# First attention batch: v's loads move to SyncE's queue, strided rows keep the mask's order, VectorE multiplies by the reciprocal sums

## The chip, the cores and the metric

The program runs on one core of one Trainium2 chip. The metric is the device time of one execution in microseconds (us); the time before is 892.8 us, the median of three runs. The engines are called TensorE (PE, with its weight loads PEld), VectorE (DVE), ScalarE (ACT), GpSimd (POOL) and SyncE (SP, which only issues transfers). The 16 DMA engines of the core are shared by all queues.

## What is computed

The reference is sparse attention followed by two MLPs, all in float32 accuracy:

```python
scores = q @ k.T / sqrt(64)                     # 4 batches, 8 heads, 576 positions, head size 64
mask_local   = (rel >= 0) & (rel < 32)          # heads 0 to 3
mask_strided = (rel >= 0) & (pos_k % 32 == pos_q % 32)   # heads 4 to 7
attn = softmax(where(mask, scores, -1e9)) @ v
x = attn as (2304 tokens, 512)
x = ((x @ w_a) * (x @ w_b)) @ w_out             # 512 -> 1536 -> 512
h = x @ w_in; y = (h * sigmoid(h)) @ w_out2     # 512 -> 2048 -> 512
```

## The kernel before, in words

**The whole.** The MLPs are a long chain of blocks on TensorE; the attention of batches 1 to 3 is woven into those blocks by a plan. Ahead of the first block stands a start-up part, which computes the attention of batch 0 alone and converts the first weights. This change touches only that part (and one tile that later batches read).

**The stages of the start-up.** A loop runs `s` from -1 upwards. The nine units of batch 0 enter one by one: units 0 to 4 are the local heads (a window of 128 positions each, the last one 64), units 5 to 8 the strided heads (`RES` lists which residues modulo 32 belong to each). In stage `s`, unit `s` gets its scores (S: TensorE, `scores`, L459 writes the mask and L466 adds q times k) and its row maxima (L: VectorE, `largest`, L488); unit `s-1` gets its exponentials (X: ScalarE, L500), 1e-9 on the sums (G: VectorE, L523) and the reciprocal and the product with it (N: `normalise`, L527 on VectorE, L538 on GpSimd); unit `s-3` is transposed (T: TensorE, L558) and copied back (U); unit `s-5` is multiplied with v (V: TensorE, `values`, L607) and stored to `x` (O: L636 on ScalarE, L639 on VectorE). `ORDER = "AXPV0QWS1LGRTBKUON2Y"` is the order of these steps inside a stage, and every engine works through its own instructions in exactly that order. Letter K puts matmuls on constants (L885) on TensorE; `WARM1` gives their number for each stage.

**Conversion of weights.** The weights come as 64-bit words of 512 KB a piece. For the first six pieces, `CONV` says in which stage a piece is converted: B (ScalarE, L701), 0 (GpSimd, L739), 1 (VectorE, L747), 2 (VectorE, L752); in the next stage Y splits it in two parts (ScalarE L774, VectorE L775). `PART` says in which stage TensorE multiplies the first half of a block with them (A, L782).

**Loads.** `LOADS` is a list by stage; capital letters go to ScalarE's queue, small ones to SyncE's, in the order written. `q`, `k` with a number are the local heads' pairs, `t8` the eight transfers of the strided q and k (L311: `qld`, `kld`, 128 bytes a row), `m7` the strided mask (six transfers L910, each a third of 54 rows, in the order of residues), `s` the sixteen transfers of the strided v (L395, tile `vs`), `w` a piece of weights (L673, L675), `u` q and k of batch 1. The local v (tile `vl`, ten transfers, L365 and L375) is issued by GpSimd in its own queue, ahead of the stage loop. Name `b` turns the strided mask into bfloat16 (L915, GpSimd), and `R` in stage 3 makes the scaled strided queries of units 5 and 6 (L427, GpSimd, six instructions).

**The order around the change.** On GpSimd, stage 3 has the mask's cast (L915), then the six query scalings, then the product of unit 2; stage 4 has that of unit 3. On VectorE, stage 4 has two transposes of the strided k (L325). On TensorE, stage 5 has the values of unit 0, the scores of unit 5, then the transpose of unit 2.

Of the kernel before, what the change touches and what calls it, by code (L numbers as in the profile page):

```python
# [9 lines left out]
F32 = mybir.dt.float32  # L10
F32R = mybir.dt.float32r
BF16 = mybir.dt.bfloat16
# [5 lines left out]
ALU = mybir.AluOpType  # L18
# [21 lines left out]

LOADS = {
    -2: (
        "q0 Q1 i M1 k0 K1 K2 Q2 t8 m7 s2 w0 s2 s1 w2 s2 s1 w1 s1 s1 s1 w4 "
        "w3 s5 u2 u5 u2"
    ),
    3: "b",
    8: "w5 w6",
    10: "w7",
    11: "w11",
    12: "w8 w9",  # L50
# [8 lines left out]
EVAC = "dada"  # L59
TURN_D = (0, 3, 5, 8)  # L60

CONV = {5: 0, 8: 1, 10: 2, 11: 3, 13: 4, 14: 5}
PART = {11: 0, 12: 1, 15: 2, 16: 3}

EARLY = len(CONV)
# [63 lines left out]
def attention_gated_mlp_silu_mlp(  # L129
# [55 lines left out]

    ident = cpool.tile([P, P], F32, name="ident")
    ident_b = cpool.tile([P, P], BF16, name="ident_b")
    lead.tile([P, 32], F32, name="lead")
    mask_loc = apool.tile([P, 4, HALF], BF16, name="mask_loc", bufs=1)
    mask_str = apool.tile([P, JR], BF16, name="mask_str", bufs=1)  # L190

# [80 lines left out]
    class Batch:  # L272
# [125 lines left out]
        def prepare(self, u):  # L398
# [20 lines left out]
            else:  # L419
                res = RES[i]  # L420
                ng = len(res)
                st = dict(w=JR, segs=2 * ng, slots=ng, n=J * (res[-1] - res[0] + TAKE))
                st["mask"] = mask_str.unsqueeze(1).to_broadcast([P, 2 * ng, JR])
                qh = queries[i % 2]
                if self.first:
                    for g, r0 in enumerate(res):
                        nc.gpsimd.tensor_scalar_mul(  # L427
                            qh[:, :, g, :JR].rearrange("p c (r j) -> p c r j", r=TAKE),
                            qT.rearrange("p c (j r) -> p c r j", r=STRIDE)[:, :, r0:r0 + TAKE],
                            SCALE,  # L430
                        )
                parts = []
# [96 lines left out]
        def normalise(self, u):  # L529
            ty, i = self.units[u]  # L530
            st = self.state[u]
            segs, w, ng = st["segs"], st["w"], st["slots"]
            rs = st["rs"]
            if self.first:
                self.invert(u)
            pr, rs = st["pr"][:, :ng, :, :w], rs.rearrange("p (i g) -> p g i", i=2)
            rs = rs.unsqueeze(3).to_broadcast([P, ng, 2, w])
            nc.gpsimd.tensor_tensor(out=pr, in0=pr, in1=rs, op=ALU.mult)  # L538

        def shared(self, us):  # L540

# [32 lines left out]
        def values(self, *us):  # L574
# [6 lines left out]
            for u in us:  # L581
                i, st = self.units[u][1], self.state[u]
                pt = st["pt"]
                for g in range(st["slots"]):
                    for k in range(2 if ty == 0 else 1):
                        for hp in range(2):
                            for c in range(2):
                                rows = slice(HALF * c, HALF * (c + 1))
                                if ty == 0:
                                    keys = slice(HALF * hp, HALF * (hp + 1))  # L590
                                    parts.append((
                                        banks[hp][rows, o + STRIDE * k:][:, :STRIDE],
                                        self.vl[keys, 2 * i + g, k, c, :],
                                        pt[keys, g, 2 * k + c, :],
                                    ))
                                else:
                                    r0 = RES[i][g]
                                    keys = slice(HALF * hp, HALF * hp + JR)
                                    out = banks[hp][rows, :first["cols"]].rearrange("p (j r) -> p r j", j=J)
                                    parts.append((  # L600
                                        out[:, r0 - RES[self.units[us[0]][1]][0]:][:, :TAKE],
                                        vs[keys, firsts.index(r0), c, :],
                                        pt[keys, P * g + HALF * c:P * g + HALF * c + JR],
                                    ))
                    o += HALF
# [270 lines left out]
    with tc.manual_schedule():  # L876
# [11 lines left out]
        nu = len(batch.units)  # L888
        every = lambda loads: [None for _ in loads]
        after = Batch(1, False)  # L890
        qs0, vs0, q1 = batch.load_qk(1), batch.load_vs(), after.load_qk(0)

        masks = [epool.tile([P, n], F32, tag="e", name="mask") for n in (5 * HALF, JR)]
        masks[0] = masks[0].rearrange("p (s k) -> p s k", k=HALF)
        nc.gpsimd.memset(masks[1], 0.0)

        def startup_loads(names):

            for name in names.split():
# [5 lines left out]
                elif name[0] == "m" and n == 1:  # L905
                    feed[0].dma_start(out=masks[0], in_=mask_loc_d)
                elif name[0] == "m":
                    for h in range(0, P, HALF):
                        for r in range(TAKE):
                            feed[0].dma_start(  # L910
                                out=masks[1][h + J * r:h + J * (r + 1)],
                                in_=mask_str_d[h:h + JR].rearrange("(j r) k -> r j k", r=TAKE)[r],
                            )
                elif name[0] == "b":
                    nc.gpsimd.tensor_copy(out=mask_str, in_=masks[1])  # L915
                elif name[0] in "qk":
                    batch.load_pair(n, "qk".index(name[0]))
                elif name[0] == "w":
                    load_words(n)
                else:  # L920
                    for _ in range(n):
                        next({"t": qs0, "s": vs0, "u": q1}[name[0]], None)

            feed[0] = nc.sync

# [3 lines left out]
        nc.gpsimd.tensor_copy(out=ident_b, in_=ident)  # L929
        for s in range(0, 4, 2):  # L930
            nc.gpsimd.tensor_copy(out=mask_loc[:, s:s + 2], in_=masks[0][:, :2])
        feed[0] = nc.gpsimd
        every(batch.load_vl())
        feed[0] = nc.sync
        keep_warm(WARM0)
        partial = {}
        for s in range(-1, max(nu + LV, max(PART), max(CONV) + 1) + 1):
# [690 lines left out]
```

## Time and profile before

| what | value |
|---|---|
| median of 3 runs | 892.8 us (892.75 to 893.99) |
| the profiled execution's own time | 891.74 us |
| its span, first to last instruction | 890.0 us |
| TensorE matmul busy | 876.0 us, 98% |
| VectorE, ScalarE, GpSimd busy | 71%, 61%, 18% |
| end of the last constant matmuls and start of solid block work on TensorE | about 44 us |

The profile is of one execution. A time in it counts from the first instruction; idle time before an instruction is written in brackets, with what ended it. When an instruction waits for several things, the one that came last by the profile is named, and a DMA can stand behind another name. [...]

### The profile page before, as it was taken

The numbers are of one execution on the slowest core, as the hardware profiler recorded it, in microseconds if no ns is written. First come the engines' busy times: TensorE is split into PE (matmuls) and PEld (weight loads), VectorE is DVE, ScalarE is ACT, GpSimd is POOL, SyncE is SP. The second block draws the span as 40 slices with busy tenths as digits, with TensorE's granted clock in tenths as the row PEclk, the third lists the DMA queues.
The fourth block names the chain that finished last, engine by engine and source line by source line (L and its number), as shares of the span: only waits on it lengthen the run. The fifth ranks groups of instructions, "written<-read, shape, count | busy, mean of one in ns | idle before, by whom it ended". The sixth has DMA issues, their size and how long they took to land.

```text
span 890.0 us, 16103 instructions
## 1 busy us (share of the span) xinstructions
PE 876.0 (98%) x5859; PEld 728.6 (82%) x5866; DVE 633.4 (71%) x1175; ACT 542.7 (61%) x1296; POOL 162.2 (18%) x232
## 2 busy tenths in 40 slices
PE   8799999999999999999999999999999999999998
PEld 5578788888887788899888888888888888898987
DVE  4687877767667665888776768776777697766664
ACT  4779898676786756675444344755554565455553
POOL 5664564444433110100000000000000000000000
PEclk9899999999999999999999999999999999999999
DMA  9999999798999922664122122321121242311201
GB/s 185 220 252 294 281 282 295 228 288 266 311 301 269 304 82 95 190 190 143 47 72 62 57 71 71 115 75 59 60 72 53 93 162 71 132 59 51 80 1 71
DMA packets 152977, 133.77 MB, mean 150 GB/s; under 512 B 91522, under 2 KB 114690, under 8 KB 152898
## 3 DMA queue, kind: packets, MB, share of 16 engines
q1 hardware_dynamic: 143986, 108.59, 43.4%
q0 software_dynamic: 7424, 23.34, 7.2%
q8 instruction: 46, 0.75, 0.3%
q10 hardware_dynamic: 1488, 0.82, 0.3%
q14 instruction: 33, 0.27, 0.1%
HBM read 110.16 MB, written 22.54 MB: 149 GB/s over the span
## 4 chain that ended last, share of the span: by engine, by line
PE 86%; DVE 5%; ACT 4%; DMA 2%; issue 1%; POOL 1%; SPq 1%; POOLq 0%; ACTq 0%; DVEq 0%
PE ring L782 17%; PE acc L1167 13%; PE ring L1103 12%; PE att L1103 9%; PE ring L1167 7%; PE att L1167 7%; PE acc L1103 7%; PE acc L1538 6%; PE acc L1566 3%; PE att L607 1%; ACT prs L500 1%; PE acc L885 1%; PE att L466 1%; DMA vs<-in_v_dram 1%; DVE w L775 1%
## 5 line engine op out<-in xcount | busy, mean ns | idle before, releaser
L1432 DVE TENSOR_TENSOR w<-raw,w 128x512 fp32r<-128x512 f32 (+1 forms) x164 | 103.2, 641 | 14.8 <-ACT w L1431 14.1
L782 PE MATMUL ring<-x1a,w 128*128 128x256 f32 (+1 forms) x480 | 99.0, 327 | 0.0
L1431 ACT CAST w<-raw 128x512 fp32r<-128x512 f32 (+1 forms) x164 | 93.1, 581 | 7.3 <-ACT w L1431 3.0
L1103 PE MATMUL ring<-L,w 128*128 128x512 f32 x360 | 87.8, 389 | 0.0
L1216 POOL DMA_DIRECT2D out_dram<-o x12 | 6.5, 543 | 407.8 <-DVE o L1215 398.9
L1103 PEld LDWEIGHTS ring<-L,w 128*128 128x128 f32 x360 | 67.6, 188 | 14.0
L1167 PE MATMUL acc<-w,h 128*128 128x512 f32 x288 | 78.5, 391 | 0.0
L782 PEld LDWEIGHTS ring<-x1a,w 128*128 128x128 f32 x480 | 71.5, 190 | 7.7
L775 DVE TENSOR_TENSOR w<-raw,w 128x512 fp32r<-128x512 f32 x80 | 61.6, 777 | 14.2 <-ACT w L774 14.1
L1538 PE MATMUL acc<-h,w 128*128 128x512 f32 x288 | 70.5, 394 | 0.6 <-ACT h L792 0.4
L792 ACT CAST h<-h 128x512 fp32r<-128x512 f32 (+1 forms) x48 | 27.2, 567 | 71.9 <-DVE h L1140 40.5
L1538 PEld LDWEIGHTS acc<-h,w 128*128 128x128 f32 x288 | 53.2, 188 | 12.4 <-ACT h L792 0.6
L1167 PEld LDWEIGHTS acc<-w,h 128*128 128x128 f32 x288 | 53.6, 188 | 9.4 <-DVE h L793 0.4
L727 POOL TENSOR_SCALAR raw<-words 128x512 f16<-128x512 uint8 x56 | 51.8, 926 | 42.5 <-DMA words<-in_moe_w_out_dram 9.8
L782 PE MATMUL ring<-x,w 128*128 128x512 f32 x240 | 58.2, 394 | 0.3 <-DVE w L775 0.3
L1167 PE MATMUL acc<-h,w 128*128 128x256 f32 (+1 forms) x288 | 53.5, 336 | 0.0
L782 PEld LDWEIGHTS ring<-x,w 128*128 128x128 f32 x240 | 44.3, 188 | 10.6 <-DVE w L775 1.6
L1167 PE MATMUL ring<-w,h 128*128 128x512 f32 x192 | 51.9, 391 | 0.0
L774 ACT CAST w<-raw 128x512 fp32r<-128x512 f32 x80 | 49.2, 623 | 1.3 <-DMA raw<-keptp 1.3
L1167 PEld LDWEIGHTS acc<-h,w 128*128 128x128 f32 x288 | 45.2, 190 | 5.7
L793 DVE TENSOR_TENSOR h<-h,h 128x512 fp32r<-128x512 f32 (+1 forms) x48 | 30.9, 643 | 26.4 <-ACT h L792 26.4
L1167 PE MATMUL att<-w,h 128*128 128x512 f32 x192 | 49.3, 391 | 0.0
(263 smaller groups left out, 1908.6 us busy)
## 6 DMA issues: line engine op xcount, KB each, us to landing
raw<-keptp SPq DMA_DIRECT2D x64, 256.0 KB
words<-in_moe_w_out_dram SPq DMA_DIRECT2D x28, 512.0 KB
raw<-kepti SPq DMA_DIRECT2D x48, 256.0 KB
raw<-kepto SPq DMA_DIRECT2D x45, 256.0 KB
words<-in_moe_w_in_dram SPq DMA_DIRECT2D x16, 512.0 KB
raw<-keptb SPq DMA_DIRECT2D x32, 256.0 KB
raw<-kepta SPq DMA_DIRECT2D x31, 256.0 KB
words<-in_moe_w_a_dram SPq DMA_DIRECT2D x12, 512.0 KB
```

What stands on the lines that cost most here:

```text
L727: nc.gpsimd.tensor_scalar(out=halves_of(made[c], F16, 1), in0=bytes_of(words[c], 8, 7), scalar1=-TINY, scalar2=127.5 * TINY, op0=ALU.mult, ...
L774: nc.scalar.copy(out=o[:, 0], in_=t)
L775: nc.vector.tensor_tensor(out=o[:, 1], in0=t, in1=o[:, 0].bitcast(F32), op=ALU.subtract)
L782: nc.tensor.matmul(ps[:, :T], lhsT=w[:, wi, c * P:(c + 1) * P], rhs=x[:, xi, c, :T], start=(c == 0 and wi == 0 and xi == 0), stop=(c == CC ...
L792: nc.scalar.copy(out=o[:, 0, :T], in_=t32[:, :T])
L793: nc.vector.tensor_tensor(out=o[:, 1, :T], in0=t32[:, :T], in1=o[:, 0, :T].bitcast(F32), op=ALU.subtract)
L1103: nc.tensor.matmul(self.acc[acc], lhsT=w[:, wi, (2 * part + c) * P:(2 * part + c + 1) * P], rhs=x[:, xi, c], start=(begin and c == 0 and m ...
L1167: nc.tensor.matmul(o, lhsT=lhsT, rhs=rhs, start=(first and wi == 0 and xi == 0), stop=(last and wi == 1))
L1431: nc.scalar.copy(out=o[:, 0, cols], in_=t)
L1432: nc.vector.tensor_tensor(out=o[:, 1, cols], in0=t, in1=o[:, 0, cols].bitcast(F32), op=ALU.subtract)
L1538: nc.tensor.matmul(accs[d], lhsT=w[:, wi, d * P:(d + 1) * P], rhs=h[:, xi], start=(j == 0 and wi == 0 and xi == 0), stop=(j == N1 - 1 and ...
L1566: nc.tensor.matmul(accs[t][:, :DM], lhsT=h[:, xi, t * P:(t + 1) * P], rhs=w[:, wi, :], start=(j == 0 and wi == 0 and xi == 0), stop=(j == ...
```

## The change

- The ten transfers of v (local heads, batch 0) leave GpSimd's queue. SyncE issues them behind the strided q and k and the mask.
- The strided mask comes in one transfer of 128 rows, in the order in which it lies in memory (position major, residue minor). It is cast into a tile `mask_first` that lies in 128 bytes a row that were an empty pad. The scaled queries of batch 0 and the columns that `values` writes follow that order.
- Later batches still want the residue-major order: in stage 8 six small transfers inside the chip (name `c`) copy the rows of `mask_first` into `mask_str` in that order.
- In batch 0 the product with the reciprocals (L538) is VectorE's instead of GpSimd's.
- The cast `b` moves from stage 3 to stage 4. Pieces 1 and 2 of the weights are converted in stages 7 and 9 instead of 8 and 10. The order of the loads of `vs` and of the weights changes: piece 1 ahead of piece 2, all of `vs` ahead of piece 2.

```diff
 LOADS = {
     -2: (
-        "q0 Q1 i M1 k0 K1 K2 Q2 t8 m7 s2 w0 s2 s1 w2 s2 s1 w1 s1 s1 s1 w4 "
-        "w3 s5 u2 u5 u2"
+        "q0 Q1 i M1 k0 K1 K2 Q2 t8 m7 v9 v1 w0 s2 s2 w1 s4 s4 s4 w2 w4 "
+        "w3 u2 u5 u2"
     ),
-    3: "b",
-    8: "w5 w6",
+    4: "b",
+    8: "w5 w6 c",
-CONV = {5: 0, 8: 1, 10: 2, 11: 3, 13: 4, 14: 5}
+CONV = {5: 0, 7: 1, 9: 2, 11: 3, 13: 4, 14: 5}
-    lead.tile([P, 32], F32, name="lead")
+    mask_first = lead.tile([P, 64], BF16, name="lead")[:, :JR]
@@ prepare
-                st["mask"] = mask_str.unsqueeze(1).to_broadcast([P, 2 * ng, JR])
+                rows = mask_first if self.first else mask_str
+                st["mask"] = rows.unsqueeze(1).to_broadcast([P, 2 * ng, JR])
-                            qh[:, :, g, :JR].rearrange("p c (r j) -> p c r j", r=TAKE),
-                            qT.rearrange("p c (j r) -> p c r j", r=STRIDE)[:, :, r0:r0 + TAKE],
+                            qh[:, :, g, :JR].rearrange("p c (j r) -> p c j r", r=TAKE),
+                            qT.rearrange("p c (j r) -> p c j r", r=STRIDE)[..., r0:r0 + TAKE],
@@ normalise
-            nc.gpsimd.tensor_tensor(out=pr, in0=pr, in1=rs, op=ALU.mult)
+            engine = nc.vector if self.first else nc.gpsimd
+            engine.tensor_tensor(out=pr, in0=pr, in1=rs, op=ALU.mult)
@@ values
-                                    out = banks[hp][rows, :first["cols"]].rearrange("p (j r) -> p r j", j=J)
+                                    out = banks[hp][rows, :first["cols"]].rearrange("p (j r) -> p j r", j=J)
+                                    out = out[..., r0 - RES[self.units[us[0]][1]][0]:][..., :TAKE]
                                     parts.append((
-                                        out[:, r0 - RES[self.units[us[0]][1]][0]:][:, :TAKE],
+                                        out if self.first else out.rearrange("p j r -> p r j"),
@@ start-up
-        nc.gpsimd.memset(masks[1], 0.0)
+        nc.gpsimd.memset(mask_str, 0.0)
                 elif name[0] == "m":
+                    feed[0].dma_start(out=masks[1], in_=mask_str_d)
+                elif name[0] == "c":
                     for h in range(0, P, HALF):
                         for r in range(TAKE):
                             feed[0].dma_start(
-                                out=masks[1][h + J * r:h + J * (r + 1)],
-                                in_=mask_str_d[h:h + JR].rearrange("(j r) k -> r j k", r=TAKE)[r],
+                                out=mask_str[h + J * r:h + J * (r + 1)],
+                                in_=mask_first[h:h + JR].rearrange("(j r) k -> r j k", r=TAKE)[r],
                             )
                 elif name[0] == "b":
-                    nc.gpsimd.tensor_copy(out=mask_str, in_=masks[1])
+                    nc.gpsimd.tensor_copy(out=mask_first, in_=masks[1])
-        feed[0] = nc.gpsimd
-        every(batch.load_vl())
-        feed[0] = nc.sync
```

## Rows read from the trace of the kernel before

**Rows 1.** Stretches: us, busy by engine, TensorE's granted clock, DMA share, GB/s.

```profile
20.00:25.00 5.00, 2.72 (x60) 1.83 (x62) 1.95 (x6) 1.59 (x7) 4.57 (x9) 1.00 0.74 204
25.00:30.00 5.00, 4.18 (x95) 2.91 (x95) 3.61 (x16) 4.15 (x26) 3.46 (x6) 0.61 0.95 214
40.00:45.00 5.00, 4.00 (x52) 2.70 (x52) 5.00 (x19) 2.68 (x11) 1.80 (x2) 1.00 1.05 254
...
54.80:97.40 42.60, 42.54 (x322) 34.02 (x322) 33.23 (x60) 37.52 (x94) 22.17 (x28) 1.00 0.99 268
```

**Rows 2.** DMA share in tenths, 10 to 26 us in 40 slices of 0.4 us.

```profile
DMA  9999999999998999999961032024469999989979
```

**Rows 3.** DMA queues, 6 to 10 us (first row), then 10 to 18 us.

```profile
q1 hardware_dynamic: 4174, 0.58, 103.9%
...
DMA packets 5598, 1.77 MB, mean 222 GB/s; under 512 B 5281, under 2 KB 5343, under 8 KB 5597
q1 hardware_dynamic: 5155, 0.65, 60.7%
q0 software_dynamic: 442, 1.10, 60.0%
```

**Rows 4.** Timeline of SyncE: start, length, line, tile, count of issues.

```profile
8.07 5.56 SPq L311 DMA_DIRECT2D kld<-in_k_dram  x4
13.75 4.01 SPq L910 DMA_DIRECT2D mask<-in_mask_str_dram  x6
18.47 1.60 SPq L395 DMA_DIRECT2D vs<-in_v_dram  x2
20.12 0.40 SPq L675 DMA_DIRECT2D words<-in_moe_w_a_dram  x1
```

**Rows 5.** Timeline of GpSimd.

```profile
7.81 5.64 POOL L375 DMA_DIRECT2D vl<-in_v_dram  x8
23.86 1.17 POOL L538 TENSOR_TENSOR prs<-prs,rs 128x256 f32<-128x256 f32 x2
25.11 0.64 POOL L739 TENSOR_SCALAR x<-words 128x512 int32<-128x512 uint8 x1
```

**Rows 6.** Timeline of ScalarE.

```profile
24.35 0.68 ACT L701 ACTIVATE e<-words 128x512 f32<-128x512 f32 x1 [2.11 <-DMA words<-in_moe_w_a_dram]
26.55 0.31 ACT L500 ACTIVATE prs<-acc,nm 128x54 f32<-128x54 f32 x1 [0.85 <-DVE nm L488]
```

**Rows 7.** Timeline of VectorE.

```profile
19.90 1.44 DVE L325 STREAM_TRANSPOSE kT<-kld 128x576 f32<-128x576 f32 x2 [1.32 <-DMA mask<-in_mask_str_dram]
25.79 0.46 DVE L747 TENSOR_SCALAR x<-words 128x512 uint8<-128x512 uint8 x1 [3.81 <-POOL x L739]
34.38 0.46 DVE L747 TENSOR_SCALAR x<-words 128x512 uint8<-128x512 uint8 x1 [1.69 <-POOL x L739]
39.74 0.46 DVE L747 TENSOR_SCALAR x<-words 128x512 uint8<-128x512 uint8 x1 [1.19 <-POOL x L739]
```

**Rows 8.** Timeline of TensorE.

```profile
19.98 0.25 PE L607 MATMUL att<-ptl,vl 64*64 64x32 f32 x2
...
21.26 1.48 PE L466 MATMUL acc<-kT,qs 64*64 64x54 f32 x24 [0.25 <-POOL qs L427]
24.51 0.44 PE L558 MATMUL ring<-ident,prs 128*128 128x128 f32 x2 [1.78 <-POOL prs L538]
...
97.60 0.73 PE L782 MATMUL ring<-x,w 128*128 128x512 f32 x2 [0.26 <-DVE w L775]
```

**Rows 9.** Groups by line and shape: count | busy us, mean ns | idle.

```profile
L639 DVE TENSOR_TENSOR x1b<-att,x1a 128x256 fp32r<-128x256 f32 x2 | 0.7, 415 | 0.0
L775 DVE TENSOR_TENSOR w<-x,w 128x512 fp32r<-128x512 f32 x4 | 2.7, 674 | 0.1
L427 POOL TENSOR_SCALAR qs<-qT 128x108 f32<-128x108 f32 x11 | 6.8, 635 | 0.1
```

**Rows 10.** Timeline of VectorE at 92 us, GpSimd reading memory at the time.

```profile
92.61 1.10 DVE L775 TENSOR_TENSOR w<-raw,w 128x512 fp32r<-128x512 f32 x1
```

More of the change, by code (lines that the diff above doesn't have):

```diff
@@ L890, in attention_gated_mlp_silu_mlp @@
         after = Batch(1, False)
-        qs0, vs0, q1 = batch.load_qk(1), batch.load_vs(), after.load_qk(0)
+        qs0, vs0, v0, q1 = batch.load_qk(1), batch.load_vs(), batch.load_vl(), after.load_qk(0)
         masks = [epool.tile([P, n], F32, tag="e", name="mask") for n in (5 * HALF, JR)]
         masks[0] = masks[0].rearrange("p (s k) -> p s k", k=HALF)
-        nc.gpsimd.memset(masks[1], 0.0)
+        nc.gpsimd.memset(mask_str, 0.0)
         def startup_loads(names):
@@ L921, in startup_loads @@
                     for _ in range(n):
-                        next({"t": qs0, "s": vs0, "u": q1}[name[0]], None)
+                        next({"t": qs0, "s": vs0, "u": q1, "v": v0}[name[0]], None)
             feed[0] = nc.sync
```

## The prediction

> **What bounds the kernel now.** I read the table by stretches first, then the timelines of the queues and engines over the first 50 us, then the ramp behind them. From 54.8 to 97.4 us TensorE is busy 42.54 of 42.60 us [rows 1], so behind the start-up the matmuls are the bound, and time can only be won ahead of them. There the worst stretch is 20 to 25 us: TensorE 2.72 of 5 us, VectorE 1.95, ScalarE 1.59, while GpSimd is busy 4.57 [rows 1]. The reader is to see three engines waiting for GpSimd and for transfers. TensorE waits 1.78 us at 24.51 for the product of unit 2 [rows 8]; VectorE waits 3.81 us up to 25.79 for the first weight's conversion on GpSimd, and ScalarE 2.11 us up to 24.35 for the first weight's transfer [rows 6, 7]. Just ahead of it the DMA engines fall nearly idle: the strip is full to 18.0 us, then at 0 to 6 tenths until 22.0 us [rows 2]. SyncE explains the hole: it is at the strided k until 13.63 us, at six tiny mask transfers until 17.76 us, and the first weight goes out at 20.12 us [rows 4]. So the start-up is a queue, not a sum of work: strided k and mask are late, GpSimd stands in order behind the mask, and the first weight is late.
>
> Later the limit changes hands. From 40 to 45 us VectorE is busy 5.00 of 5 [rows 1].
>
> **Part 1, v behind q and k on SyncE.** Removed from GpSimd: ten issues, of which the last eight take 5.64 us from 7.81 [rows 5]. GpSimd has nothing else then (its next work waits for the first reciprocal), so this is worth nothing. What counts is the order of the transfers. The strided q and k are 9,216 pieces of 128 bytes (2 tensors, 4 heads, 576 rows, two halves). With SyncE's queue nearly alone, 4,174 packets moved from 6 to 10 us, 1,044 a microsecond; with v beside it, 5,155 in 8 us, 644 a microsecond, while v's queue took 60.0% of the engines' time [rows 3]. Behind the change the second part goes at the first rate: 5,155 / 1,044 = 4.9 us, done at 14.9 us, instead of running to the thin end of the strip at 18.4 [rows 2]. The gain in k itself is small, because VectorE came to its transposes only at 18.6 us and began them at 19.90, after 1.32 us of waiting [rows 7]; the three products that it now does before them (1.2 us, priced below) eat that.
>
> v is 1.18 MB. At the mean 222 GB/s of 10 to 18 us [rows 3] it takes 5.3 us: drained at 20.2, landed at 20.2 to 21.7 (the last k was used 1.5 us after the strip thinned out at 18.4 [rows 2, 7]); I take 21.0. TensorE began unit 0's values at 19.98 [rows 8], so this is a new wait of 1.0 us. Queued behind it on TensorE: scores of unit 5, transpose of unit 2. Both wait less than before: unit 5's matmuls took 1.48 us at 21.26 because the scaled queries came in drops, and the 1.78 us for the product are gone [rows 8]. From the values' start to unit 5's first matmul it took 1.28 us, 0.25 of them waiting [rows 8]. So 21.0 + 1.0 + 1.2 (estimate: the 1.48 less the drops) = 23.2, and the transpose starts there instead of at 24.51: the new wait is covered by 1.3 us. The cover is gone if v lands after 22.3.
>
> **Part 2, one mask transfer.** Five issues and their room in the queue go, 4.01 us from 13.75 [rows 4]. With them goes the hole: v and the weight stand right behind. The first weight (0.52 MB) at the 214 GB/s of 25 to 30 us [rows 1] takes 2.5 us behind v: 22.7, landed at 23.2 with 0.5 us for the landing (bounds: 21.3 with v and weight at the 268 GB/s of the ramp and no tail, 24.8 with both at the 204 GB/s of 20 to 25 us and a tail of 1.5 [rows 1]). It was used at 24.35 [rows 6].
>
> **Part 3, the cast and the queries on GpSimd.** Six scalings at 0.635 us [rows 9] from VectorE's second query transpose (about 18.1, an estimate: just ahead of its idle time that began at 18.58 [rows 7]) end at 21.9, then the narrow cast, some 0.2: 22.1. The scores of unit 5 want that at about 21.7, a loss of 0.4 us that the cover above holds. The new pattern of the scaling has runs of 3 instead of 18; no row shows its price. Bounds: 0.64 x 108/512 = 0.14 us from the 512-wide conversion [rows 5], and twice 0.635; I take 0.635. The slow bound would put the scores at 25.9 and take the gain away.
>
> **Part 4, products on VectorE.** GpSimd loses them, so the first conversion no longer stands behind 1.17 us of products; it started at 25.11 [rows 5] and can start at 23.3, when the weight is there. VectorE's next step, at 25.79 [rows 7], then starts at 23.3 + 0.64 + 0.06 = 24.0. **Main term: 25.79 - 24.0 = 1.8 us** (bounds 0.3 to 3.8 by the landing of the weight). Unit 5's maxima stand right behind it on VectorE, and ScalarE's exponentials of unit 5, at 26.55 [rows 6], move with them. The price on VectorE: 415 ns for 256 columns, 674 ns for 512 [rows 9], so about 1.0 ns a column and 0.16 fixed: 0.42 x 4 + 0.29 + 0.49 x 3 + 0.38 = 3.8 us for nine, of which five, 2.1 us, fall after 25 us. They go into idle time: VectorE waits 1.69 us at 34.38 and 1.19 us at 39.74 for conversions that stood behind products on GpSimd [rows 7], 2.9 us together. ScalarE is near solid behind 26.55 (4.15 of 5 from 25 to 30 [rows 1]) and caps what is won. Net 0.8 by VectorE; I count **0.5 us** (bounds -2.1, if neither wait shrinks, to 0.8).
>
> **Part 5, the rest.** Pieces 1 and 2 convert a stage earlier: same instructions, ahead of VectorE's full stretch; 0. Their new order in the queue puts piece 2 behind all of `vs`, but everything in the queue is some 3 us earlier (the hole); 0. Six small copies in stage 8 are issues on SyncE at 0.67 us each (4.01 / 6 [rows 4]), 4 us at most, when its next weights are for pieces converted stages later; 0, covered by those stages. Memset and pad: 0.
>
> **Sum.** 1.8 + 0.5 = 2.3 us, kept to the end: VectorE's full stretch from 40 us only begins earlier, and behind it TensorE is full [rows 1]. Against the profiled execution 891.74 - 2.3 = 889.4; the median lies 1.06 above that execution, so 890.5.
>
> **The rivals.**
>
> *Given back in the ramp.* TensorE waited 0.26 us at 97.60 for a split [rows 8], and from 54.8 to 97.4 the DMA share is 0.99 and ScalarE works 37.52 of 42.60 us [rows 1]. If weights can't come earlier, blocks that begin 2.3 us earlier wait there: 892.8 less at most 0.5, 892.5. Against it: the hole is filled, so transfers come earlier too.
>
> *VectorE pays.* Each of the seven products beside GpSimd work may also be held up by a reading instruction there, as the split was: 1.10 - 0.67 = 0.43 us each, 3.0 us in all, and VectorE is full from 40 us [rows 1]. Gain 2.3 - 3.0 = -0.7: 893.5. The split's 1.10 us against 674 ns [rows 9, 10] speak for it; against it, the waits on GpSimd at 34.38 and 39.74 are larger than the products. The Trainium skill, "SBUF — State Buffer", section "Who interferes with whom", states the rule behind it: a VectorE instruction with two SBUF inputs contends with a GpSimd instruction that reads SBUF, and whichever comes second waits for the whole of the other. By that rule, the sum is the 893.5 of this rival if every product comes second, and the 890.5 of the forecast if none does; the slow split agrees with it.
>
> *v late (slower).* Place: values of unit 0, at the head of TensorE's order, with the weight behind v in the same queue. If v's 4,608 pieces of 256 bytes go at 500 a microsecond instead of 870 (1.18 MB at 222 GB/s), v takes 9.2 us and drains at 24.1, the weight lands at 27.1 and VectorE's step starts at 27.8: 2.0 us late, 0.5 won later: 892.8 + 1.5 = 894.3. It decides from v drained at 22.1 us on (then the step starts at 25.79), 640 pieces a microsecond, which is the rate of the contested stretch [rows 3]. Against it: there is no second queue then.
>
> *More.* The granted clock was 0.61 of full, so partly at 1.2 GHz, from 25 to 30 us, right behind TensorE's 2.72 busy of 5 [rows 1]. If the gap is small enough that it stays at 2.4 GHz, matmuls of that stretch come up to 2 us earlier (39% of 5 us), capped by ScalarE's idle time there (0.85 of those 5 us, and an estimated 0.65 more to 35 us) at 1.5: 892.8 - 3.8 = 889.0.
>
> **How the numbers follow.** Forecast 0.50 (its own range 889.0 to 892.0), more 0.14, given back 0.14, VectorE pays 0.08, v late 0.14. A change of 0.2% is 1.8 us, about what this measurement can tell from none. Faster: 0.39 of the forecast and all of "more", 0.53. Same: 0.11 of the forecast, 0.14 given back, 0.04 of "VectorE pays": 0.29. Slower: 0.14 and 0.04, 0.18. The range of 8 in 10 takes the forecast, the greater part of "more" and the two cases around no change: 888.2 (the best bounds of the two terms, 3.8 + 0.8) to 893.4.
>
> **What would show it.** Right: the strip full without a hole to 23 us; the first weight used at 23.2 us; VectorE's L747 at about 24.0; the transpose of unit 2 with no wait for a product; VectorE's waits at the second and third L747 under half. Wrong: TensorE idle over 2 us ahead of L607 near 20 us, or the first weight after 24.3; or these right and a longer wait near 95 us.

## The result, and the profile after

The changed kernel took 900.5 us (median of 4 runs, 898.1 to 902.9) against 893.05 us: a ratio of 1.0077, 95% interval 1.0056 to 1.0097. It is slower by 5 to 8.7 us; the prediction said 890.5. The profiled execution took 900.68 us with a span of 898.9 us (before 891.74 and 890.0), so 8.9 us more are to be found in it. From L420 on, line numbers have moved by 1 to 5; the tiles' names are the same, and `lead` is the tile that `mask_first` lies in. Weights are counted by piece: the first is `w0`, the third `w2`, the sixth `w5`.

Stretches of the changed kernel, columns as in [rows 1]:

```profile
15.00:20.00 5.00, 4.54 (x97) 2.66 (x98) 4.66 (x17) 3.62 (x23) 1.47 (x3) 1.00 0.53 116
20.00:25.00 5.00, 1.54 (x14) 1.03 (x14) 2.13 (x7) 1.02 (x5) 1.68 (x5) 0.73 0.68 148
25.00:30.00 5.00, 4.31 (x80) 2.86 (x81) 0.81 (x4) 1.16 (x5) 1.41 (x3) 0.59 0.95 227
30.00:35.00 5.00, 4.15 (x90) 2.80 (x91) 4.83 (x19) 5.00 (x31) 2.78 (x5) 1.00 0.42 81
...
60.00:65.00 5.00, 5.00 (x15) 4.00 (x16) 3.65 (x7) 4.21 (x8) 2.57 (x4) 0.68 1.09 255
```

The worst stretch has got worse: TensorE 1.54 of 5 us instead of 2.72 [rows 1]. From 25 to 30 us VectorE and ScalarE, which had 3.61 and 4.15 us of work there, stand nearly still at 0.81 and 1.16. And the DMA engines have two holes: a share of 0.53 from 15 to 20 us and 0.42 from 30 to 35 us, where the kernel before had 0.84 and 0.77.

DMA share from 10 to 26 us in 40 slices (against [rows 2]), and the queue from 10 to 18 us (against [rows 3]):

```profile
DMA  9499999999724012396977930005969799953999
```

```profile
DMA packets 6953, 1.08 MB, mean 134 GB/s; under 512 B 6951, under 2 KB 6951, under 8 KB 6951
...
q1 hardware_dynamic: 6951, 1.04, 77.2%
```

The strided k drains early, as forecast: the strip is full to 14 us. But v doesn't follow at 222 GB/s: there are holes from 14.4 to 16.8 us (mean share 0.27) and from 19.2 to 20.8 us (0.14), where the queue had little but v left to carry. SyncE's timeline says why (against [rows 4]):

```profile
12.42 0.77 SPq L911 DMA_DIRECT2D mask<-in_mask_str_dram  x1
13.23 1.88 SPq L365 DMA_DIRECT2D vl<-in_v_dram  x2
15.15 6.98 SPq L375 DMA_DIRECT2D vl<-in_v_dram  x8
22.17 0.63 SPq L678 DMA_DIRECT2D words<-in_moe_w_a_dram  x1
...
25.06 9.58 SPq L395 DMA_DIRECT2D vs<-in_v_dram  x12
34.69 0.44 SPq L678 DMA_DIRECT2D words<-in_moe_w_a_dram  x1
...
36.30 6.63 SPq L311 DMA_DIRECT2D qld<-in_q_dram  x4
43.03 3.16 SPq L311 DMA_DIRECT2D kld<-in_k_dram  x4
46.30 2.23 SPq L678 DMA_DIRECT2D words<-in_moe_w_a_dram  x1
...
49.14 4.58 SPq L915 DMA_DIRECT2D mask_str<-lead  x6
```

The mask is one issue of 0.77 us, but the ten issues of v take 8.9 us, from 13.23 to 22.13 (0.60 to 1.09 us each, and one of 2.25). So the first weight, which was issued at 20.12 us [rows 4], goes out at 22.17. Then twelve loads of `vs` stand in a row for 9.58 us, and the third weight behind them goes out at 34.69 us. In the kernel before the same two weights were issued so (SyncE's timeline of the kernel before, third and sixth weight):

```profile
21.82 0.51 SPq L675 DMA_DIRECT2D words<-in_moe_w_a_dram  x1
...
40.56 0.62 SPq L675 DMA_DIRECT2D words<-in_moe_w_a_dram  x1
```

The sixth weight is 5.7 us later. GpSimd, ScalarE and VectorE of the changed kernel show both delays:

```profile
28.52 0.64 POOL L742 TENSOR_SCALAR x<-words 128x512 int32<-128x512 uint8 x1 [6.83 <-DMA words<-in_moe_w_a_dram]
...
51.90 0.66 POOL L742 TENSOR_SCALAR x3a<-words 128x512 int32<-128x512 uint8 x1 [7.25 <-DMA words<-in_moe_w_a_dram]
```

```profile
28.84 0.67 ACT L704 ACTIVATE e<-words 128x512 f32<-128x512 f32 x1 [6.82 <-DMA words<-in_moe_w_a_dram]
```

```profile
29.19 0.47 DVE L750 TENSOR_SCALAR x<-words 128x512 uint8<-128x512 uint8 x1 [6.98 <-POOL x L742]
...
38.49 0.88 DVE L540 TENSOR_TENSOR prs<-prs,rs 128x324 f32<-128x324 f32 x1
...
52.59 0.47 DVE L750 TENSOR_SCALAR x3a<-words 128x512 uint8<-128x512 uint8 x1 [3.93 <-POOL x3a L742]
```

VectorE's first conversion step, 25.79 us before [rows 7] and forecast for 24.0, stands at 29.19. The wait names GpSimd, and GpSimd's row names the weight's transfer.

TensorE's first out-block (twelve matmuls of `h` with a piece of `w_out`) in the kernel before:

```profile
54.05 0.51 PE L1538 MATMUL acc<-h,w 128*128 128x512 f32 x1 [0.40 <-ACT h L792]
54.78 2.84 PE L1538 MATMUL acc<-h,w 128*128 128x512 f32 x11 [0.22 <-DVE h L793]
```

In the changed kernel, TensorE at the values of unit 0 (19.98 us before [rows 8]) and then at the first out-block:

```profile
22.19 0.38 PE L610 MATMUL att<-ptl,vl 64*64 64x32 f32 x2 [1.81 <-DMA vl<-in_v_dram]
...
25.32 0.31 PE L610 MATMUL acc<-ptl,vl 64*64 64x32 f32 x1 [0.78 <-DMA vl<-in_v_dram]
...
57.35 0.30 PE L467 MATMUL att<-kT,qT 64*32 64x64 f32 x4 [2.57 <-DVE kT L325]
...
59.23 0.50 PE L1540 MATMUL acc<-h,w 128*128 128x512 f32 x1 [0.40 <-ACT h L795]
59.96 4.30 PE L1540 MATMUL acc<-h,w 128*128 128x512 f32 x11 [0.22 <-DVE h L796]
```

The account by the offset to the kernel before:

- 3.4 us at VectorE's first conversion step.
- 5.2 us at the first out-block (59.23 against 54.05). VectorE waits 3.93 us for the sixth weight's conversion and comes to its transposes of the second batch's q and k only behind it, without waiting for their transfers.
- 6.7 us at the second out-block (69.56 against 62.91). The first ran at a granted clock of 0.68 in that stretch, partly 1.2 GHz, behind 5 us in which TensorE was busy for 1.67, and its eleven matmuls took 4.30 us instead of 2.84.
- 7.6 us at 118.71 us, after short waits of TensorE (0.31 us at 73.26, 0.54 at 111.99).
- 8.6 to 8.9 us from 273 us to the end, after the wait of ScalarE that the last section shows.

### The profile page after: what moved, and what is told of

The parts are those of the page before. It is cut to its first block, busy times and chain, and to the rows that moved or that the text cites. A ratio compares the mean times of both kernels' runs of the same rounds, so it can differ in the third digit from the quotient of the medians.

```text
span 898.9 us, 16088 instructions
## 1 busy us (share of the span) xinstructions
PE 878.5 (98%) x5859; PEld 730.5 (81%) x5866; DVE 636.6 (71%) x1184; ACT 542.9 (60%) x1296; POOL 147.8 (16%) x213
## 4 chain that ended last, share of the span: by engine, by line
PE 80%; DMA 6%; SPq 5%; ACT 3%; DVE 3%; issue 2%; POOL 1%; POOLq 0%; DVEq 0%; ACTq 0%
PE ring L785 16%; PE acc L1169 13%; PE ring L1105 12%; PE att L1105 9%; PE ring L1169 7%; PE att L1169 7%; PE acc L1105 7%; PE acc L1540 4%; PE acc L1568 3%; DMA words<-in_moe_w_b_dram 3%; DMA raw<-kepti 1%; ACT prs L501 1%; SPq L311 1%; SPq L375 1%; PE att L610 1%
## 5 line engine op out<-in xcount | busy, mean ns | idle before, releaser
L704 ACT ACTIVATE e<-words 128x512 f32<-128x512 f32 x68 | 44.8, 659 | 11.7 <-DMA words<-in_moe_w_a_dram 11.2
```

Source lines behind the costliest of these rows:

```text
L704: nc.scalar.activation(out=e.bitcast(F32), in_=high.bitcast(F32), func=AF.Copy, scale=REBASE)
```

## Experiments

Each ratio is against the kernel before on the same chip, with its 95% interval; one thousandth is 0.9 us. In the order strings `v` is v, `w` a weight, `s` loads of `vs`, `u` loads of the second batch's q and k, `c` the six copies. The experiments are numbered as they ran and told in the order of the argument.

**1. v back in GpSimd's queue** (the changed kernel otherwise).

```diff
-  "... t8 m7 v9 v1 w0 s2 s2 w1 s4 s4 s4 w2 w4 w3 u2 u5 u2"
+  "... t8 m7 w0 s2 s2 w1 s4 s4 s4 w2 w4 w3 u2 u5 u2"
+        feed[0] = nc.gpsimd
+        every(batch.load_vl())
+        feed[0] = nc.sync
         keep_warm(WARM0)
```

> The changed kernel with the ten transfers of v put back into GpSimd's queue, all else as changed. Theory A (v in SyncE's queue is the cause: SyncE needs 8.9 us to issue it, it lands at 25.3 us, and everything behind it in that queue is late): TensorE's values of unit 0 start near 20 us without a wait, the first weight is used before 25 us, time 890 to 893. Theory B (the six copies and the new order of weights and strided v make the sixth weight late): the sixth weight is still used after 50 us and the time stays above 896. Theory C (VectorE's products): time stays above 896 with VectorE behind from 30 us on.

Measured 1.0006 (0.9989 to 1.0024), 894.3 us: the whole loss is gone with this one edit, as theory A had it, but no gain is left (A had 890 to 893). The first weight goes out at 18.05 us and VectorE's first conversion step stands at 22.96 us, 2.8 us ahead of the kernel before; the first out-block is only 0.6 us ahead, and later ones 1.6 us behind.

**2. The kernel before with v alone moved to SyncE**, behind `t8 m7`.

> The kernel before with one thing changed: v issued by SyncE behind strided q, k and the six mask transfers. Theory A: 6 to 10 us slower than before (899 to 903), with v landing after 25 us. Theory B and C: within 2 us of before, because the order of the weights and the products are as before.

Measured 1.0018 (1.0000 to 1.0036), some 1.6 us. v is late in the same way (2.19 us of waiting at the values of unit 0, first conversion step at 27.86 us), but the sixth weight goes out at 42.93 us, 2.4 us late and not 5.7. So v starts the loss, and the rest of the change makes it larger. Theory A's 6 to 10 us for v alone are missed, and the interval's lower end is no loss at all.

**3. The six copies issued by GpSimd** (`nc.gpsimd.dma_start` for `c`), v on SyncE.

> The changed kernel with the six small copies of the mask issued by GpSimd instead of SyncE. They hold SyncE from 49.1 to 53.7 us. Theory A: they stand behind the sixth weight's issue, so its lateness stays; a gain of 0 to 1.5 us (899 to 900.5) through the pieces behind them. Theory B: 3 us or more faster (below 897.5).

Measured 1.0044 (1.0026 to 1.0062), 3 us better than the change, with 2.4 us to either side (an estimate from the two intervals). The first out-block is still 5.0 us late, but the offset stays there (4.6 at 124.56 us).

**4. The first weight ahead of v**, `m7 w0 v9 v1`.

> The changed kernel with the first weight's transfer ahead of v in SyncE's queue. It separates the two things that are late at 20 to 29 us. If the first weight's lateness (used 28.8 instead of 24.4 us) sets VectorE's and ScalarE's pace, the start-up's stage 6 begins up to 3 us earlier and the time falls by 1 to 3 us. If v's lateness at TensorE's head sets it (values of unit 0 end at 26.1), nothing is won: within 1 us of the changed kernel, with v some 2 us later still.

Measured 1.0048 (1.0026 to 1.0069). The first weight isn't waited for, v is (3.82 us), and the sixth weight goes out at 44.75 us. The time is 2.6 us below the change, within the first branch's 1 to 3 us, but with 2.7 us to either side it doesn't exclude the second branch. Three fifths of the loss are left with the weight first.

**5. The old order of `vs` and weights behind v** (the string before the change, with `v9 v1` behind `m7`).

> The changed kernel whole, v on SyncE, but behind v the small pieces vs and the weights go out in the old order (two vs, first weight, two vs, one vs, third weight ...) instead of the new one. Theory 1 (v in SyncE's queue starts the loss, and the new order, with all twelve vs ahead of pieces 2, 4 and 3, adds to it): the sixth weight is issued earlier than 46.30 us, the first out-block starts 1 us or more before 59.23 us, and the time is 897 to 899. Theory 2 (v and the six copies alone make the loss; the order of the rest doesn't matter, since the number of issues is the same): the sixth weight at 46 us again, 900 to 901.

Measured 1.0040 (1.0027 to 1.0052): 3.3 us better, sixth weight issued at 44.46, first out-block at about 56.6 us. The new order had its own price.

**6. v and the copies on GpSimd**, new order kept.

> The changed kernel with v issued by GpSimd again, and the six copies of the mask's strided rows issued by GpSimd too, so that SyncE has neither. With v back alone, the first out-block started at 53.45 us (0.6 before the kernel before) but was 1.6 us behind it from the second stretch of out-blocks on. Theory 1 (the six copies on SyncE, with the slow clock and the late weights behind them, cost that): out-blocks stay 0.6 us or more ahead of the kernel before to the end, 891 to 893 against 893 for the kernel before. Theory 2 (the products on VectorE and the sixth weight, no earlier than before, cost it): as with v back alone, 894 to 895.

Measured 1.0003 (0.9989 to 1.0016). Still no gain, with VectorE's first conversion step at 23.11 us. The first theory missed, and the second one's 894 to 895 came; the next lines that matter are of the DMA engines, in experiment 13.

**7. Two weights ahead of the second batch's q and k**, otherwise as 6: `8: "w5 w6 u2 u5 u2 c"`.

> As the kernel with v and the copies on GpSimd, and also the sixth and seventh weight ahead of the second batch's q and k in SyncE's queue. Theory 1 (the 1.8 us won ahead of VectorE's first conversion is given back because SyncE's queue brings the sixth weight at 46 us, no earlier than before): GpSimd no longer waits 6 us for it, the first out-block starts at 51 to 52.5 us instead of 53.45, and the time is 889.5 to 892. Theory 2 (the stretch is bound elsewhere, by VectorE or by the second batch's q and k, which now come later): a wait for the second batch's q and k takes its place, 893 to 896.

Measured 1.0011 (0.9996 to 1.0025). The sixth weight goes out at 30.95 us and GpSimd converts it at 38.38 instead of 46.08, but the second theory's wait takes its place on VectorE:

```profile
51.97 1.44 DVE L325 STREAM_TRANSPOSE kT<-kld 128x576 f32<-128x576 f32 x2 [3.15 <-DMA kld<-in_k_dram]
```

**8. The kernel before with the products alone on VectorE.**

```diff
-            nc.gpsimd.tensor_tensor(out=pr, in0=pr, in1=rs, op=ALU.mult)
+            engine = nc.vector if self.first else nc.gpsimd
+            engine.tensor_tensor(out=pr, in0=pr, in1=rs, op=ALU.mult)
```

> The kernel before with one edit: the nine products of the first batch's normalising on VectorE instead of GpSimd. Theory 1 (they fit into VectorE's idle time, as the prediction had it, and the first weight still sets VectorE's first conversion): the conversion no longer stands behind 1.17 us of products on GpSimd, no change by more than 0.1%, 892 to 894. Theory 2 (VectorE pays: products held up beside GpSimd and VectorE full from 40 us): 895 to 897.

Measured 0.9998 (0.9982 to 1.0015): VectorE doesn't pay, and by itself the edit gains nothing.

**9. Old order and copies on GpSimd**, v on SyncE (5 and 3 together).

> The changed kernel with v on SyncE, the old order of vs and weights behind it, and the six copies issued by GpSimd. Theory 1 (the loss is the sum of three loads on one queue: v some 2 us, the six copies some 3, the new order some 3): what is left is v's part, 894.5 to 896.5, the sixth weight issued at 43 to 45 us, the first out-block 2 to 2.6 us behind the kernel before and still no more than that at 115 us. Theory 2 (the three don't add, each removal takes back the same microseconds): 897 to 899, as with the old order alone or the copies alone.

Measured 1.0034 (1.0018 to 1.0050), 897.0 us. That lies just between the two theories; the profiled execution was the fastest of ten (893.5 us), so its rows don't decide. The two edits together take back 3.8 us; the 3.3 and 3.0 that each takes back alone would add up to 6.3. The difference of 2.5 us is within its noise of 3 us, so whether these prices add stays open.

**10. Half of v in the same ten issues.** The eight longer ones load 4 windows instead of 8 or 9; VectorE sets the rest of the tile to zero in the first 3.3 us.

```diff
-                n = (S - k0) // HALF
+                n = (S - k0) // HALF // (2 if self.first else 1)
```

> The changed kernel with the same ten issues of v on SyncE, but the eight longer ones load only 4 of their 8 or 9 windows of 64 rows (the rest of v is zero, so the first batch's values are not the reference's). Theory 1 (the ten issues themselves take SyncE's time): the issues end at 20.5 to 22.5 us again, the first weight goes out right behind them, and v's last piece is used at 23.5 us or later. Theory 2 (SyncE is held up because v's 256-byte pieces move slowly and the queue is full): the issues end by 18 us and the first weight goes out 4 us earlier.

SyncE's timeline, and the DMA share from 10 to 18 us in 40 slices:

```profile
14.70 6.58 SPq L377 DMA_DIRECT2D vl<-in_v_dram  x8
21.32 0.60 SPq L680 DMA_DIRECT2D words<-in_moe_w_a_dram  x1
```

```profile
DMA  7999999999999999941005110004301930840661
```

With half the data the eight issues take 6.58 us instead of 6.98, the weight goes out at 21.32 us, and the DMA engines stand idle for most of 13.5 to 17 us. So SyncE is held by the issues themselves, not by the bytes. v's last piece is used at 23.16 us, 0.3 earlier than the first theory's bound and 2.2 earlier than with all of v; VectorE's first step stands at 26.63 us, 2.6 earlier. The sixth weight still goes out at 44.62 us, 4.1 later than in the kernel before, and most of the loss is left: 1.0063 (1.0041 to 1.0086). So the late landing of v is not what costs most.

**14. Ten tiny loads of 2 KB in v's former place**, v on GpSimd as in 1.

```diff
+    tiny = apool.tile([P, 10, 4], F32, name="tiny", bufs=1)
...
+                elif name[0] == "d":
+                    for r in range(n):
+                        feed[0].dma_start(out=tiny[:, r], in_=mask_str_d[:, :4])
```

> The changed kernel with v back on GpSimd, and at v's former place in SyncE's queue ten tiny loads (2 KB each, into a tile that nothing reads). Theory 1 (what v costs on SyncE is the time of ten issues, whatever they carry): the first weight goes out 6 us later than the 18.05 us of the kernel with v on GpSimd, the sixth at 45 us or later, 897 to 901, most of the changed kernel's loss. Theory 2 (v's own bytes, or its values landing late, make the loss): 894 to 895.5, as with v on GpSimd.

SyncE's timeline, and a stretch (columns as in [rows 1]):

```profile
17.56 5.68 SPq L922 DMA_DIRECT2D tiny<-in_mask_str_dram  x10
23.28 0.43 SPq L679 DMA_DIRECT2D words<-in_moe_w_a_dram  x1
...
45.59 0.83 SPq L679 DMA_DIRECT2D words<-in_moe_w_a_dram  x1
```

```profile
20.00:25.00 5.00, 3.41 (x95) 2.40 (x95) 2.32 (x7) 1.20 (x7) 1.87 (x5) 1.00 0.22 27
```

Measured 1.0074 (1.0053 to 1.0096), where the changed kernel has 1.0077 and experiment 1, without the tiny loads, 1.0006. v isn't on SyncE here, and TensorE doesn't wait for it; 20 KB in ten issues make the whole loss. The DMA engines have a share of 0.22 from 20 to 25 us while SyncE is busy issuing. This settles it: the loss is the time of ten issues in a queue that everything later stands in.

**15. The kernel before with the new order alone.**

> The kernel before with one edit: the new order of vs and weights (first weight ahead of vs, then four, and twelve in a row ahead of the third, fifth and fourth weight). Theory 1 (the twelve vs in a row leave the DMA engines idle, and the weights behind them are late): DMA share below 0.6 somewhere between 25 and 35 us instead of 0.95 and 0.77, 894.5 to 897. Theory 2 (the order costs only together with v on the same queue): 892.5 to 894.

Measured 1.0002 (0.9990 to 1.0014). The hole is there (DMA share 0.48 and 0.54 from 25 to 35 us, before 0.95 and 0.77), and over twelve runs it costs nothing that can be measured. The signs are of the first theory, the time is nearer to the second. In the profiled execution (895.8 us, where the median is 894.2) the sixth weight goes out at 43.30 us and the first out-block stands at 56.81, 2.8 us late. Why the time doesn't follow isn't shown; one reading is that the kernel before has no earlier first step that the hole could spoil.

**13. v and copies on GpSimd, and the old order.** What is left of the change is the one mask transfer, the new row order and the products on VectorE.

> The changed kernel with v and the copies issued by GpSimd and also the old order of vs and weights: all that is left of the change is the one mask transfer, the new row order, and the products on VectorE. Theory 1 (with the new order, twelve vs in a row leave the DMA engines idle from about 27 to 31 us, and this hole is what takes back the microseconds won ahead of VectorE's first conversion): the DMA share of 25 to 30 us is 0.8 or more instead of 0.48, the first out-block starts at 51.5 to 53 us, 889.5 to 892 against 893.5. Theory 2 (the prediction's main term is worth nothing, since the transfers of this stretch take as long in any order): first out-block at 53 to 54 us, 893 to 895.

Measured 0.9973 (0.9958 to 0.9988), 891.7 us: **faster than both kernels, than the kernel before by 2.4 us (0.0027 of 893.7; 2.0 by the medians).** SyncE, GpSimd and VectorE:

```profile
13.67 3.99 SPq L911 DMA_DIRECT2D mask<-in_mask_str_dram  x1
17.70 0.75 SPq L395 DMA_DIRECT2D vs<-in_v_dram  x2
18.50 0.40 SPq L678 DMA_DIRECT2D words<-in_moe_w_a_dram  x1
```

```profile
23.64 0.65 POOL L742 TENSOR_SCALAR x<-words 128x512 int32<-128x512 uint8 x1 [2.70 <-DMA words<-in_moe_w_a_dram]
```

```profile
24.32 0.46 DVE L750 TENSOR_SCALAR x<-words 128x512 uint8<-128x512 uint8 x1 [1.72 <-POOL x L742]
```

The stretch from 25 to 30 us, first of experiment 6 (new order), then of 13 (old order):

```profile
25.00:30.00 5.00, 4.34 (x121) 2.78 (x113) 4.82 (x18) 5.00 (x30) 4.18 (x8) 1.00 0.48 88
```

```profile
25.00:30.00 5.00, 3.94 (x87) 2.86 (x89) 4.28 (x16) 5.00 (x31) 2.07 (x4) 0.81 1.02 261
```

With twelve `vs` in a row the DMA engines carry 88 GB/s, with weights among them 261. In both VectorE's first step is early (23.11 and 24.32 us), but the first out-block follows in full only in 13, at 52.33 us against 53.40 in 6 and 54.05 before:

```profile
53.40 4.20 PE L1543 MATMUL acc<-h,w 128*128 128x512 f32 x12
```

```profile
52.33 0.49 PE L1543 MATMUL acc<-h,w 128*128 128x512 f32 x1 [0.40 <-ACT h L795]
```

These rows tell of the start-up alone: by their whole time the two profiled executions go the other way, 891.2 us for 6 (the fastest of its twelve) and 893.9 for 13.

**16. The new order with the weights spread**, `w0 s2 s2 w1 s2 s2 w2 s2 s2 w4 s2 w3 s2 u2 u5 u2`, v and copies on GpSimd.

> The kernel with v and the copies on GpSimd, and an order that keeps the first weight ahead of vs but has the other weights between them, two vs at a time. Theory 1 (the hole in the transfers is what takes the gain back): no hole, first out-block at 51 to 52.5 us, 889 to 892. Theory 2 (worth nothing): 893 to 895.

Measured 0.9976 (0.9962 to 0.9991), 892.5 us: as fast as 13, first conversion step at 23.04 us, first out-block at 51.18 us, DMA share 0.90 from 25 to 30 us. What has to be kept is weights among the `vs`, not the old order.

**11 and 12. The second batch's q and k issued by GpSimd in stage 8**, two weights ahead on SyncE; 11 on top of 6 (with the copies at stage 13), 12 on the kernel before.

> The changed kernel with v on GpSimd, and also the second batch's q and k (eight issues) on GpSimd behind its second weight conversion, so that the sixth and seventh weight go out on SyncE at 31 us; the six copies on GpSimd at stage 13. Theory 1 (the 1.8 us won ahead of VectorE's first conversion is given back because SyncE's queue brings the sixth weight, or else the second batch's q and k, too late): neither waits now, the first out-block starts at 51 to 52.5 us, 890 to 892 against 893.3. Theory 2 (the second batch's q and k still come too late for their transposes, or GpSimd's conversions are late behind the issues): first out-block at 53 us or later, 893 to 895.

> The kernel before with only the order of the queues changed in the same way: the second batch's q and k issued by GpSimd in stage 8, the sixth and seventh weight ahead of them. Theory 1 (SyncE's queue is what sets the first out-block in the kernel before too): the sixth weight goes out at 31 us, first out-block at 52 to 53.5 us instead of 54.05, 891 to 892.5. Theory 2 (VectorE's late first conversion sets it): no change, 893 to 894.

Measured 1.0022 (1.0006 to 1.0039) and 1.0045 (1.0028 to 1.0062): both misses. In 11 GpSimd waits for a weight that went out at 30.01 us and is used at 43.97, beside the q and k that GpSimd now issues from 28.34 to 35.23 us:

```profile
43.97 0.65 POOL L743 TENSOR_SCALAR x<-words 128x512 int32<-128x512 uint8 x1 [8.01 <-DMA words<-in_moe_w_b_dram]
```

In 7 and 11 issuing one transfer earlier made another late. In 12 the price is GpSimd's own time: it issues from 35.05 to 41.62 us, its products and its conversion stand behind, and VectorE waits for that conversion. The first out-block stands at 60.40 us.

```profile
38.38 3.24 POOL L311 DMA_DIRECT2D kld<-in_k_dram  x4
41.65 1.25 POOL L538 TENSOR_TENSOR prs<-prs,rs 128x324 f32<-128x324 f32 x2
```

```profile
43.66 0.47 DVE L747 TENSOR_SCALAR x<-words 128x512 uint8<-128x512 uint8 x1 [3.94 <-POOL x L739]
```

So a queue on another engine isn't free either: the issues take the time of whatever stands behind them there.

## Why the prediction was wrong

**The step that failed is Part 2's "v and the weight stand right behind", with Part 1's 5.3 us for v.** It moved v by its bytes, 1.18 MB at 222 GB/s, and had no term for SyncE's own time in ten issues, though a price stood in the rows: eight took GpSimd 5.64 us [rows 5], 0.7 each. On SyncE ten took 8.9 us, so the weight that was to be used at 23.2 us went out at 22.17 and was used at 28.84. Experiments 10 and 14 show that bytes don't set SyncE's time or the loss: half of v takes it 8.6 us, and ten tiny loads make the same loss. The prediction's own signs of being wrong both came: the first weight after 24.3, and TensorE idle for 3.7 us in all within the values of unit 0.

v's bytes have a smaller part, in the first step alone. From its issue to its use by ScalarE the first weight took 6.7 us behind all of v, 4.9 behind half of it (10), and 4.2 both behind the tiny loads (14) and in the kernel before. The 222 GB/s came from a stretch in which v moved in GpSimd's queue, 1.10 MB in 442 packets [rows 3]; in SyncE's queue all but 2 of the packets from 10 to 18 us are under 512 B.

**The rival "v late" named the right place and the wrong reason and size.** TensorE waited at the values of unit 0, v's last piece came at 25.3 us, VectorE's step at 29.2 (the rival had 24.1 and 27.8). But it made the lateness a rate of pieces, and with half of the pieces SyncE's issues end only 0.85 us earlier (10), while the DMA engines stand idle; and it ended its sum at that step, +1.5. The loss was 7.5, because the same queue carries everything later.

**Part 5 failed twice.** "Everything in the queue is some 3 us earlier" was the reverse: the first weight was 2 us later, the sixth 5.7. The new order, priced at 0, cost 3.3 us with v on SyncE (experiment 5) and took back all of the gain without it (6 against 13, 1.0003 against 0.9973). The six copies, priced at 0 under cover of "pieces converted stages later", cost about 3 us (3); without v and its delay they cost nothing that can be measured (1 against 6).

**The main term's number came, in part by another route.** Without v on SyncE, copies and the new order (13), VectorE's first step stands at 24.32 us (forecast 24.0), and the kernel is 2.4 us faster (forecast 2.3). Of the 1.47 us at that step, 1.07 came as Parts 3 and 4 said: before, GpSimd reached the weight 0.76 us behind ScalarE (25.11 and 24.35), because products stood ahead; now it waits for the transfer alone and is 0.31 ahead of it (23.64 and 23.95). The other 0.40 us are the weight's earlier landing by ScalarE's use, and here Part 2 was wrong once more. With v in GpSimd's queue the single mask issue takes 3.99 us and ends at 17.66 us, where six of them ended at 17.76; it takes 3.2 to 4.2 us in experiments 1, 6, 7, 11, 14 and 16 too. So Part 2's 4.01 us were not won. What is gone in 13 are two waits of SyncE for the strided k behind the mask, in the kernel before (us in total, times, longest):

```profile
SPq L395 <- DMA kld<-in_k_dram: 1.7, 2, 1.0
```

So the first weight goes out at 18.50 us instead of 20.12. That the forecast, with v on SyncE and the mask's time won, and experiment 13, with neither, both come to about 24 us is luck. What Parts 1 and 5 added, priced at little or nothing, took the gain away.

**Smaller steps.** k is done early, as forecast, at about 14 us for 14.9. The scalings took 529 ns on average, so shorter runs cost nothing (635 was taken). The products took 0.42, 0.29, 0.50 and 0.39 us, as priced, and VectorE's second and third conversion steps wait under 0.2 us where they waited 1.69 and 1.19 [rows 7]. "VectorE pays" is excluded by experiment 8: seen once, at 38.49 us, where a product took 0.88 instead of 0.50 us beside a conversion on GpSimd. The rule of the Trainium skill, "SBUF — State Buffer", section "Who interferes with whom", agrees with that row. Two products beside scalings that had begun 0.34 us before them, at 19.34 and 30.75 us, kept their 0.42 and 0.29 us, so the rule's full wait isn't borne out there. In all it cost 0.4 us. (In experiment 13 one product took 0.90 us in the same way.)

**Open.** v on SyncE costs 1.6 us in the kernel before (2) and 6 in the changed one (1 against the change). The runs show the parts on which this depends, but not how they share it. Nor is it shown why SyncE's single issues take as long as they do, the long ones above all.

## What to carry to other kernels

Price a moved transfer twice: by its bytes on the DMA engines, and by its issues on the queue that it joins. Here they took 0.60 to 1.09 us each for v (one 2.25), 0.43 for 2 KB (one 1.40) and 0.43 to 0.63 for the 512 KB weight right behind them, so bytes don't tell the price. Then walk that queue to its end, since the late one that costs most may be the last in line. An issue removed saves its time only if the engine isn't then held by the next thing in line, as here by the strided k. Where many small issues stand ahead of large transfers, try the large ones among them, since the DMA engines ran empty here while the queue was busy; and when several moves come in one change, run it without each, as the gain may be in the part that was left in place.

## What the runs showed of the hardware

- A queue that issues without a pause can leave the DMA engines idle: ten 2 KB loads took 5.68 us (0.43 each and one of 1.40), with a DMA share of 0.22 around them; v's ten, eight of them of 128 and 144 KB, took 8.9 us, and with half the data 8.6. Among v's issues one took 2.25 us; the kernel before has such a long one too, the first of its six mask issues (2.26 us). Where v is in GpSimd's queue, the one mask issue behind the strided k is the long one, 3.2 to 4.2 us; where v stands behind it on SyncE, it took 0.6 to 2.2. The cause wasn't found.
- The granted clock can stay low through work that looks solid: in experiment 15 TensorE was busy 4.78 of 5 us at 0.50 of full, 1.2 GHz, from 25 to 35 us, behind a stretch with 2.69 busy of 5. Such a row shows less work done than its busy time says: 88 matmuls in 4.78 us from 25 to 30 us, where the kernel before did 95 in 4.18 at 0.61 [rows 1].
- A second wait, far behind the change, adds its own microseconds to any version. ScalarE's split of a weight that is read back from memory, at 261 to 274 us, waits for that transfer; the row is of the changed kernel, then of experiment 13:

```profile
273.18 0.62 ACT L777 CAST w<-raw 128x512 fp32r<-128x512 f32 x1 [1.39 <-DMA raw<-kepti]
```

```profile
264.65 0.62 ACT L777 CAST w<-raw 128x512 fp32r<-128x512 f32 x1 [2.73 <-DMA raw<-kepti]
```

The kernel before has no such wait in its profiled execution. In that of 13 it takes back the 2.3 us by which an out-block at 108.84 us had been ahead (111.10 before), and the execution took 893.9 us where the median is 891.7. The kernel before ranges over 5 to 7 us on one chip (890.3 to 897.6 us over 34 runs), which a single profile can't average.
